# Attention, mixture of experts and a second feed-forward on one core: C's maxima kept in PSUM, 1e-9 as the second addend of a sum, A's factor inside its multiplication, and new priorities

## The chip, the cores and the metric

The kernel runs on one core of a Trainium2 chip. The metric is device microseconds (us) of one execution, and the number to be predicted is the median of the runs of the changed kernel. The engines are TensorE (PE; its weight loads are PEld), VectorE (DVE), ScalarE (ACT), GpSimd (POOL) and SyncE (SP), which issues most of the DMAs. Every engine works through its own list of instructions in order.

## The reference, cut to what matters

Three parts run one after the other. The first is an attention with 32 landmarks per head, over 4 batches of 8 heads, 576 tokens and 64 columns:

```python
q_lm, k_lm = means of q and k over groups of 18 tokens      # 32 landmarks each
def sm(a, b):
    s = scale * a @ b.T
    e = np.exp(s - s.max(-1))
    return e / (e.sum(-1) + 1e-09)
A, Bm, C = sm(q, k_lm), sm(q_lm, k_lm), sm(q_lm, k)
Z = six Newton steps from Bm.T / (norms + 1e-6)             # an inverse of Bm
x = A @ Z @ C @ v
```

The result is one row of 512 per token. The second part gives each of the 2304 rows to the best of 8 experts (512 to 1024, relu, back to 512), scaled by the gate's probability, and an expert takes at most 576 rows. The third part is a feed-forward from 512 to 2048 and back with a slope alpha for negative values.

## The kernel before, in words

**Stages.** The attention is worked on in pieces of one batch b and half of the heads g (four heads, 128 partitions), eight pieces in all. For each piece `loads`, `turn` and `sums` fetch q and k, turn them on PE and form the landmarks; `attend_c` makes C, B and the product with v; `attend_a` makes A. `attention_post` then inverts B with six Newton steps on PE and DVE (tiles `RW`), first for batch 0 alone (`post0`), then for batches 1 to 3 together (`post`), and ends in `route`, which gives every row its expert and writes `table`. When batch 0's logits `L` are known, `first_expert` writes the number of an expert into `e0i`, and `weights` loads that expert's matrices with that number (tiles `W1` and `W2`, both shown as `W` in the profile). `landmark_rows` multiplies W1 by the landmark rows (`big<-W,MT` on PE) and splits the product into two 16-bit halves (`MW`).

**First pass and loop.** The first pass, written out in full, is `moe_h` (PE: `mm<-xT,MW`), `moe_y` (`mm<-W,hgA`), `moe2_h` (`mm<-yA,WIa` and `mm<-yB,WIa`) and `moe2_out` (`mm<-WO,hgA`, `mm<-WO,hgB`). Meanwhile the third part's 64-bit weights are narrowed (DVE, three instructions a pair of chunks: `WIa<-hgA`, `WIb<-st`, `W<-st`, `MW<-st`, `xT<-st`) and split (`WIa<-WIa,s_wi`, then `WO<-W,s_wo`). `experts` makes a list of the (batch, expert) pairs that are left (`x_lst`), and a loop runs the same four steps for each; the profile shows two turns of it.

**What sets the order.** Every sequence of operations is a stream with a rank. `Plan.run` picks, with costs of its own for every instruction, the operation that can start first; a stream of smaller rank may go ahead within `patience + EAGER * difference of ranks`. What comes out is one fixed order on each engine. Where the plan sees PE wait, `keep_warm` puts matmuls of zeros on PE's list ahead of the waiting work (tiles `zero` and `ones`; L1730 in the profile; below: fillers). They are part of the program: PE runs them whether or not the wait comes.

**What the change touches.** In `attend_c` (L673) the two maxima go into `mx`, are multiplied by `exps` into `nm2`, and ACT's two exponentials write their sums into `sums`; then 1e-9 is added (`rs<-sums`) and the reciprocal taken. In `attend_a` (L736) the sums of A go into `asum`, one instruction adds 1e-9 and multiplies by 1/64, then come the reciprocal and the multiplication of T1 (`T<-T,asum`). `moe_tiles` (L1134) makes the long-lived tiles, `mtn` among them, which the first `prefetch` writes. The numbers are at L25, L210 and in the calls that make streams. GpSimd's subtraction for the 16-bit remainder of A is the POOL instruction `parts<-AT,parts`.

Of the kernel before, what the change touches and what calls it, by code (L numbers as in the profile page):

```python
# [11 lines left out]
AF = mybir.ActivationFunctionType  # L12
ALU = mybir.AluOpType
AX = mybir.AxisListType
# [3 lines left out]
P = 128  # L18
# [6 lines left out]
RANKS = [[-190.251, -162.415], [-189.669, -24.286], [-21.570, 79.087], [95.553, -68.442]]  # L25
# [6 lines left out]
MUL = "dddddddd"  # L32
# [172 lines left out]
class Plan:  # L205
# [5 lines left out]
    EAGER = -23.848  # L211
# [173 lines left out]
class Kernel:  # L385
# [41 lines left out]
    def constants(self):  # L427
# [29 lines left out]
        self.streams["constants"].own = -182.905  # L457
# [72 lines left out]
    def loads(self):  # L530

        for b in range(self.B):
            for g in range(2):
                heads = slice(4 * g, 4 * g + 4)
                self.streams["loads"].own = RANKS[b][g] + -135.434
                for nm, src in (("k", self.k), ("q", self.q)):
                    self.raw[nm, b, g] = t = yield Get(self.S["qk"])
                    yield self.dq.dma_start(t, src[b, heads].rearrange("h (p j) d -> (h p) j d", j=TG))
                    self.have.add((nm, b, g))
                if (b, g) == (0, 0):  # L540
                    self.streams["values"] = yield Fork(self.values(), -141.457)

    def values(self):

        for b in range(self.B):
            for g in range(2):
                heads = slice(4 * g, 4 * g + 4)
                if (b, g) != (0, 0):
                    self.streams["values"].own = RANKS[b][g] + -72.894
                self.raw["v", b, g] = t = yield Get(self.S["v"])  # L550
                src = self.v[b, heads]
                yield self.dq.dma_start(t[:, :, :4].rearrange("p h t d -> p h (t d)"), src[:, : 4 * P].rearrange("h (p t) d -> p h (t d)", t=4))
                yield self.dq.dma_start(t[:64, :, 4], src[:, 4 * P :].rearrange("h p d -> p h d"))
                self.have.add(("v", b, g))
                if (b, g) == (0, 0):
                    self.tc.prologue_barrier()

    def sums(self):
# [3 lines left out]
        for b in range(self.B):  # L562
            for g in range(2):
                self.streams["sums"].own = RANKS[b][g] + -193.537
# [24 lines left out]
    def turn(self):  # L589
# [8 lines left out]
        for b in range(self.B):  # L598
            for g in range(2):
                self.streams["turn"].own = RANKS[b][g] + -168.287  # L600
# [71 lines left out]
    def attend_c(self, b, g):  # L672
# [4 lines left out]
        def t(name, n):  # L677
            return self.ap.tile([P, n], F32, tag=name, name=f"{name}{b}{g}", bufs=dict(sums=4, rs=4, EB=3).get(name, 2))
# [7 lines left out]
        mx, nm2, sums, rs, EB = t("mx", 2), t("nm2", 2), t("sums", 2), t("rs", 2), t("EB", 32)  # L686
# [5 lines left out]
        yield act.activation(EC.rearrange("p (m j w) -> p m j w", m=LM, w=2), turned, AF.Exp, bias=nm2[:, 0:1], scale=0.125 / TG, accum_out=sums[:, 0:1])  # L692
        yield act.activation(EB, landmarks, AF.Exp, bias=nm2[:, 1:2], scale=0.125 / TG**2, accum_out=sums[:, 1:2])
        yield Put(big)
        yield dve.tensor_scalar(rs, sums, 1e-9, None, op0=ALU.add)
# [38 lines left out]
    def attend_a(self, b, g):  # L734
# [15 lines left out]
        amx, asum = t("amx", 18), t("asum", 18)  # L750
# [16 lines left out]
        self.streams["store", b, g] = yield Fork(self.store(b, g, parts), -169.245)  # L767
# [8 lines left out]
    def attention_post(self, bs):  # L776
# [79 lines left out]
        if b == 0:  # L856
            self.streams["post0"].own = -65.619
# [53 lines left out]
        for n, bb in enumerate(bs):  # L911
# [18 lines left out]
            if bb == 0:  # L930
                yield from self.first_expert(L[0:1, 0, 0, :])
                self.streams["post0"].own = -141.092
            yield Fork(self.used(bb, AT))
        self.have.add(("x", bs[-1]))
        if b:
            yield self.until(("routed", 0))
            self.streams["post"].own = -137.701
# [37 lines left out]
    def route(self, bs, L):  # L975
# [82 lines left out]
        if b == 0:  # L1058

            i0 = self.ar.tile([P, 5], F32, tag="r_i0", name="r_i0")  # L1060
            yield dve.scalar_tensor_tensor(i0, code[:, 0], self.e0c, row[:, 0], op0=ALU.is_equal, op1=ALU.mult)
            yield dve.tensor_scalar(self.idx0, i0, float(self.NT), None, op0=ALU.add)
            self.have.add("idx0")
            self.streams["post0"].own = 87.367
# [68 lines left out]
    def moe_tiles(self):  # L1133
# [12 lines left out]
        self.mtn = t("mtn", [P, 2, 2, 32])  # L1146
        self.gate, self.gn = t("gate", [P, self.B, 5]), t("gn", [P, 5])
# [55 lines left out]
    def landmark_rows(self, MT, slots, late=0.0):  # L1203
# [26 lines left out]
        scale = yield Fork(self.scale_of("w1", 4), -169.035)  # L1230
# [38 lines left out]
    def early(self):  # L1269
# [12 lines left out]
        self.streams["early_loads"] = yield Fork(loads(), 95.023)  # L1282
# [42 lines left out]
    def convert(self, name, n, amax=None, low="d", load=None, first=0):  # L1325
# [9 lines left out]
        scale = yield Fork(self.scale_of(name, n // 2, amax), -176.626)  # L1335
# [12 lines left out]
    def weight2(self, name, src, amax, low, first=0):  # L1348
# [9 lines left out]
        if name == "wi":  # L1358
            self.streams["wi_loads"] = yield Fork(self.fetch(name, src, range(first, 16, 2), arrived), -164.840)
        else:  # L1360
            self.streams["wo_loads"] = yield Fork(self.fetch(name, src, range(first, 16, 2), arrived), -192.828)
# [248 lines left out]
    def pre(self):  # L1610

        yield self.until(("P", 0, 0), ("P", 0, 1), *([("used", self.n_early - 4)] if self.n_early else ["early"]))
        self.streams["first"].own = -176.600
# [4 lines left out]
        self.streams["first"].own = -137.454  # L1618
# [3 lines left out]
        self.streams["first"].own = -135.600  # L1622
# [3 lines left out]
    def weights(self):  # L1626
# [4 lines left out]
        self.streams["rows"] = yield Fork(self.landmark_rows(self.MT[:, 0:2], [self.big] * 2), -69.061)  # L1631
        yield self.until("early")
        self.streams["weights"].own = -23.924
        yield from self.load_expert(bass.ds(e0, 1), ["w2"])
        self.streams["weights"].own = -139.397
# [85 lines left out]
    def run(self):  # L1721
# [15 lines left out]
        with tc.manual_schedule(engines={ET.PE, ET.DVE, ET.Activation, ET.Pool, ET.SP}):  # L1737
# [24 lines left out]
            for _ in range(10):  # L1762
# [5 lines left out]
                "constants": Stream(self.constants(), -68.342),  # L1768
                "post0": Stream(self.attention_post([0]), -168.986),
                "first": Stream(self.pre(), -79.218),  # L1770
                "weights": Stream(self.weights(), 79.632),
                "rooms": Stream(self.rooms(), -66.559),
                "post": Stream(self.attention_post(list(range(1, self.B))), -164.819),
                "early": Stream(self.early(), 71.164),
                "wi": Stream(self.weight_in(), -75.754),
                "wo": Stream(self.weight_out(), -66.781),
                "clear": Stream(self.clear(), -178.670),
                "experts": Stream(self.experts(), -70.639),
                "out": Stream(self.first_out(), -183.331),
                "next": Stream(self.first_next(), -135.603),  # L1780
                "next_w1": Stream(self.next_w1_late(), -193.387),
                "next_w2": Stream(self.next_w2('d'), -168.460),
            }
            for b in range(self.B):
                for g in range(2):
                    self.streams["c", b, g] = Stream(self.attend_c(b, g), RANKS[b][g] + -75.228)
                    self.streams["a", b, g] = Stream(self.attend_a(b, g), RANKS[b][g] + 80.769)
# [41 lines left out]
```

## Time and profile before

| | |
|---|---|
| median of 3 runs | 524.16 us (523.25 to 524.59) |
| the profiled execution | 524.16 us, of which the span in the trace is 519.9 us |
| busy in the span | PE 503.6 us, DVE 299.4 us, ACT 259.4 us, POOL 88.8 us |
| matmuls of zeros (L1730) | 174 in the first pass |
| first pass on PE | up to 248.13 us; then two turns of the loop, at 248.13 and 381.74 us |
| granted PE clock | 0.998 of full speed |

A profile names an instruction by the line that issued it, which is L81 for all that the plan orders, and by its tiles. The page's first part gives busy time by engine, the table of windows gives it by stretch of time, and a row of the timeline gives start, duration, engine, operation and, in brackets, the idle time ahead of it with what ended it.

### The profile page before, as it was taken

How to read it: one execution, taken by the hardware profiler on the slowest of the kernel's cores; microseconds unless marked ns; L12 is line 12 of the kernel's file. 1: busy time of each engine (PE TensorE's matmuls, PEld its weight loads, DVE VectorE, ACT ScalarE, POOL GpSimd, SP SyncE). 2: the span in 40 equal slices, each digit the busy share in tenths (PEclk: the TensorE clock that was granted, in tenths of full speed). 3: DMA queues.
4: the chain of work that ended last, by engine and by line, in shares of the span. 5: the costliest groups of instructions: out<-in, count | busy, mean ns of one | idle time of the engine just before them, and what ended most of it. 6: DMA issues, size and time to landing. Idle time of an engine off the chain costs nothing.

```text
span 519.9 us, 12146 instructions
## 1 busy us (share of the span) xinstructions
PE 503.6 (97%) x4809; PEld 332.0 (64%) x4809; DVE 299.4 (58%) x712; ACT 259.4 (50%) x579; POOL 88.8 (17%) x139
## 2 busy tenths in 40 slices
PE   8999999999989999999999999999999999999995
PEld 6777867776576774444755868644575587774444
DVE  6888989989999988024422657900033356682000
ACT  5666575774687676533522568700132255881000
POOL 4979401010134332011100000000100000000001
PEclk9999999999999999999999999999999999999999
DMA  8897597526553596500013570000000249000000
GB/s 309 303 331 244 172 276 264 182 103 223 151 143 143 185 308 207 202 34 29 33 20 52 155 242 0 1 21 20 20 30 0 50 94 317 3 0 2 38 20 32
DMA packets 50682, 64.47 MB, mean 124 GB/s; under 512 B 20320, under 2 KB 34032, under 8 KB 50640
## 3 DMA queue, kind: packets, MB, share of 16 engines
q1 hardware_dynamic: 49536, 60.34, 36.8%
q0 software_dynamic: 1104, 3.54, 1.8%
q8 instruction: 30, 0.49, 0.4%
q14 instruction: 12, 0.10, 0.1%
HBM read 49.50 MB, written 10.62 MB: 116 GB/s over the span
## 4 chain that ended last, share of the span: by engine, by line
PE 79%; DVE 9%; issue 6%; DMA 4%; ACT 1%; POOL 0%; POOLq 0%; SPq 0%; ACTq 0%; DVEq 0%
PE mm L81 73%; PE big L81 4%; PE mm L1730 2%; DVE WIa L81 2%; DMA out<-st,idxc 2%; DVE W L81 1%; DVE MW L81 1%; DMA st<-in_moe_w_out 1%; DVE mm L81 1%; DVE hgA L81 1%; DMA qk<-in_k 1%; DVE g L81 1%; ACT st L81 0%; PE big L1730 0%; ACT MW L81 0%
## 5 line engine op out<-in xcount | busy, mean ns | idle before, releaser
L81 PEld LDWEIGHTS <-hgA 128*128 128x128 f16 (+1 forms) x864 | 70.5, 102 | 69.2 <-issue 6.2
L81 PEld LDWEIGHTS <-WIa 128*128 128x128 f16 x864 | 84.2, 98 | 28.2 <-issue 6.7
L81 PE MATMUL mm<-WO,hgA 128*128 128x512 f16 (+1 forms) x432 | 72.8, 344 | 0.0
L81 PE MATMUL mm<-W,hgA 128*128 128x512 f16 (+1 forms) x432 | 72.7, 344 | 0.2
L81 PE MATMUL mm<-WO,hgB 128*128 128x512 f16 (+1 forms) x432 | 72.8, 344 | 0.0
L81 PE MATMUL mm<-yB,WIa 128*128 128x320 f16 x432 | 61.5, 299 | 1.8 <-DVE hgA L81 1.2
L81 POOL DMA_INDIRECT out<-st,idxc x12 | 12.3, 1028 | 287.9 <-ACT st L81 282.8
L81 PEld LDWEIGHTS <-hgB 128*128 128x128 f16 (+1 forms) x432 | 35.3, 102 | 36.1 <-issue 3.3
L81 ACT ACTIVATE st<-mm,fac 128x512 f32<-128x512 f32 (+1 forms) x15 | 9.7, 644 | 97.6 <-PE mm L81 97.4
L81 PE MATMUL mm<-yA,WIa 128*128 128x256 f16 x432 | 50.6, 272 | 2.3 <-DVE g L81 1.7
L81 ACT ACTIVATE g<-mm 128x256 f32<-128x256 f32 (+1 forms) x96 | 39.2, 413 | 20.9 <-PE mm L81 14.8
L81 DVE SCALAR_TENSOR_TENSOR mm<-g,oma,mm 128x256 f32<-128x256 f32 (+1 forms) x80 | 40.9, 517 | 8.2 <-ACT g L81 7.5
L81 PE MATMUL mm<-xT,MW 128*128 128x320 f16 (+1 forms) x288 | 37.0, 286 | 1.8 <-ACT st L81 1.8
L81 PEld LDWEIGHTS <-MW 128*128 128x128 f16 x288 | 27.6, 98 | 9.3 <-ACT st L81 1.4
L81 PEld LDWEIGHTS <-WIb 128*128 128x128 f16 x288 | 28.2, 99 | 7.1 <-issue 0.2
L81 ACT ACTIVATE junk<-mm 128x512 bf16<-128x512 f32 (+1 forms) x27 | 15.5, 573 | 34.4 <-PE mm L81 34.2
L81 DVE COPY idxc<-idxn 128x5 int32<-128x5 int32 x2 | 0.3, 172 | 54.9 <-issue 43.9
L81 ACT COPY qkT<-mm 128x512 f32<-128x512 f32 (+1 forms) x48 | 22.6, 525 | 17.1 <-PE mm L81 17.0
L81 ACT ACTIVATE junk<-W 128x1024 bf16<-128x1024 f32 x21 | 22.2, 1055 | 8.7 <-DMA W<-in_moe_w 8.2
L81 ACT ACTIVATE hgA<-mm 128x256 f16<-128x256 f32 (+1 forms) x48 | 19.5, 409 | 13.7 <-PE mm L81 13.4
L81 DVE TENSOR_TENSOR hgA<-mm,hgA 128x256 f16<-128x256 f32 (+1 forms) x40 | 18.2, 455 | 14.1 <-ACT hgA L81 13.3
L81 DVE SCALAR_TENSOR_TENSOR hgA<-mm,hgA 128x256 f16<-128x256 f32 (+1 forms) x48 | 20.9, 454 | 7.5 <-ACT hgA L81 7.3
(286 smaller groups left out, 751.5 us busy)
## 6 DMA issues: line engine op xcount, KB each, us to landing
W<-in_moe_w SPq DMA_DIRECT2D x8, 1024.0 KB, 8.6
st<-in_moe_w_out SPq DMA_DIRECT2D x16, 512.0 KB, 4.3
hgA<-in_moe_w_in SPq DMA_DIRECT2D x10, 512.0 KB, 6.9
qk<-in_k SPq DMA_DIRECT2D x8, 576.0 KB, 5.4
qk<-in_q SPq DMA_DIRECT2D x8, 576.0 KB, 6.4
out<-zero SPq DMA_DIRECT2D x18, 256.0 KB, 4.3
v<-in_v SPq DMA_DIRECT2D x8, 512.0 KB, 5.4
W<-in_moe_w SPq DMA_DIRECT2D x8, 512.0 KB, 5.6
```

Source lines behind the costliest of these rows:

```text
L81: r = getattr(self.lane.engine, name)(*a, **k)
L1730: nc.tensor.matmul(o[:, :256], self.ones16, self.zero.bitcast(F16), start=True, stop=True)
```

## The change

C: both maxima are written into two unused columns of the same PSUM tile (`SC[:, 1008:1010]`), and the multiplication reads them there. The sums of C, and those of A, go into the first place of pairs whose second place holds 1e-9, written once at the start into `mtn`; a `tensor_reduce` over each pair then adds it. A: the factor 64 goes into the multiplication of T1, which becomes a `scalar_tensor_tensor`. All ranks, `RANKS` and `EAGER` have new values.

```diff
-RANKS = [[-190.251, -162.415], [-189.669, -24.286], [-21.570, 79.087], [95.553, -68.442]]
+RANKS = [[-158.429, -51.160], [-190.869, -58.900], [-50.798, 57.716], [-188.686, -53.152]]
-    EAGER = -23.848
+    EAGER = -192.112
...
-        mx, nm2, sums, rs, EB = t("mx", 2), t("nm2", 2), t("sums", 2), t("rs", 2), t("EB", 32)
+        nm2, rs, EB = t("nm2", 2), t("rs", 2), t("EB", 32)
+        mx, sums = SC[:, 1008:1010], self.sums2[:, 2 * b + g]
...
-        yield act.activation(EC.rearrange("p (m j w) -> p m j w", m=LM, w=2), turned, AF.Exp, bias=nm2[:, 0:1], scale=0.125 / TG, accum_out=sums[:, 0:1])
+        yield act.activation(EC.rearrange("p (m j w) -> p m j w", m=LM, w=2), turned, AF.Exp, bias=nm2[:, 0:1], scale=0.125 / TG, accum_out=sums[:, 0, 0:1])
...
-        yield dve.tensor_scalar(rs, sums, 1e-9, None, op0=ALU.add)
+        yield dve.tensor_reduce(rs, sums, axis=AX.X, op=ALU.add)
         yield dve.reciprocal(rs, rs)
...
-        yield dve.tensor_reduce(asum, T13, axis=AX.X, op=ALU.add)
-        yield dve.tensor_scalar(asum, asum, 1e-9, 1.0 / ASCALE, op0=ALU.add, op1=ALU.mult)
+        yield dve.tensor_reduce(asum2[:, :, 0], T13, axis=AX.X, op=ALU.add)
+        yield dve.tensor_reduce(asum, asum2, axis=AX.X, op=ALU.add)
         yield dve.reciprocal(asum, asum)
-        yield (dve if MUL[2 * b + g] == "d" else self.gp).tensor_tensor(T13, T13, asum.unsqueeze(2).to_broadcast([P, 18, 32]), op=ALU.mult)
+        yield dve.scalar_tensor_tensor(T13, T13, ASCALE, asum.unsqueeze(2).to_broadcast([P, 18, 32]), op0=ALU.mult, op1=ALU.mult)
...
+        eps = self.mtn.rearrange("p g k m -> p (g k m)")[:, :104]
+        self.nc.vector.memset(eps, 1e-9)
+        self.asum2 = eps[:, :72].rearrange("p (g n a) -> p g n a", g=2, a=2)
+        self.sums2 = eps[:, 72:].rearrange("p (g n a) -> p g n a", n=2, a=2)
...
-                "weights": Stream(self.weights(), 79.632),
+                "weights": Stream(self.weights(), -189.922),
```

The new numbers move most instructions of the first pass, on every engine; the loop's order is the same but for two instructions near its end. Two places bear on the prediction. The first is on DVE, where the first logits are copied (`L`) and the first expert's number is written (`e0i`). Before, `AT` tiles of batch 2 are being made there and the row stands 121st of DVE's rows:

```order
L81 COPY L_1135<-mm_1136 128x40
L81 TENSOR_SCALAR rs_1128<-sums_1127 128x2
...
L81 SCALAR_TENSOR_TENSOR WIa<-hgA,WIa 128x1024
L81 TENSOR_REDUCE m_1265<-d_1266 1x1
L81 STREAM_TRANSPOSE AT_1288<-T_5_966 128x576
L81 TENSOR_SCALAR e0i<-m_1265 1x1
L81 TENSOR_REDUCE r_mx_1337<-L_1135 128x5
```

Of the changed kernel, at the same two instructions (`T_8` is the last of the eight pieces of A, `Bn` the three later batches' B):

```order
L80 COPY L_1401<-mm_1402 128x40
...
L80 TENSOR_REDUCE m_1452<-d_1453 1x1
L80 STREAM_TRANSPOSE T_8_1387<-big_1433 128x576
L80 TENSOR_SCALAR e0i<-m_1452 1x1
L80 TENSOR_REDUCE rsum_1515<-Bn_131 128x6
L80 TENSOR_SCALAR a_1483<-a_1483 1x1
L80 TENSOR_REDUCE amx_1510<-T_8_1387 128x18
```

The first expert's number now comes behind nearly all of the attention's DVE work, 147th instead of 121st of the rows.

The second place is on DVE in the first `moe2_h`, from the second activated product on (`mm<-g,oma,mm` and `g<-g,oma,mm` are the products' slopes, `hgA` their low halves, `W<-st` a narrowing of w_out, `WIa<-WIa,s_wi` a split of w_in). Before:

```order
L81 SCALAR_TENSOR_TENSOR g_2_2660<-g_2_2660,oma,mm_2640 128x256
L81 SCALAR_TENSOR_TENSOR xh_2548<-mm_2497,pys,xh_2548 128x2x256
...
L81 TENSOR_TENSOR hgA<-mm_2613,hgA 128x256
L81 SCALAR_TENSOR_TENSOR WIa<-WIa,s_wi 128x2x512
L81 SCALAR_TENSOR_TENSOR mm_2676<-g_3_2692,oma,mm_2676 128x256
L81 COPY x_n<-mm_2679 32x2
L81 SCALAR_TENSOR_TENSOR W_86<-st_6_2468,W_86 128x1024
L81 SCALAR_TENSOR_TENSOR g_4_2714<-g_4_2714,oma,mm_2697 128x256
```

Of the changed kernel, from the same product (`SS` and `tsum` belong to the routing of batches 1 to 3):

```order
L80 SCALAR_TENSOR_TENSOR g_2_2625<-g_2_2625,oma,mm_2604 128x256
...
L80 TENSOR_SCALAR W_86<-st_7_2489 128x1024
L80 TENSOR_TENSOR tsum<-tsum,SS 128x8
...
L80 TENSOR_TENSOR hgA<-mm_2589,hgA 128x256
L80 SCALAR_TENSOR_TENSOR mm_2638<-g_3_2654,oma,mm_2638 128x256
L80 SCALAR_TENSOR_TENSOR g_4_2686<-g_4_2686,oma,mm_2661 128x256
L80 CAST SS<-tsum 128x8
L80 SCALAR_TENSOR_TENSOR W_86<-st_7_2489,W_86 128x1024
```

The splits of w_in now stand ahead of the stretch, and in their place stand small instructions of the later batches' routing, which before stood ahead of it.

## Rows read from the trace of the kernel before

**Rows 1.** The page's part 1: busy time by engine.

```profile
PE 503.6 (97%) x4809; PEld 332.0 (64%) x4809; DVE 299.4 (58%) x712; ACT 259.4 (50%) x579; POOL 88.8 (17%) x139
```

**Rows 2.** Windows: stretch and length, then busy PE, PEld, DVE, ACT, POOL, clock, DMA.

```profile
0.00:52.00 52.00, 49.02 (x786) 37.99 (x786) 41.92 (x96) 32.32 (x83) 39.12 (x95) 1.00 0.86 297
52.00:97.00 45.00, 43.49 (x798) 33.72 (x798) 41.44 (x116) 26.68 (x65) 8.34 (x9) 1.00 0.70 230
97.00:144.00 47.00, 47.00 (x606) 31.32 (x604) 45.10 (x111) 31.88 (x61) 4.77 (x3) 1.00 0.53 167
144.00:210.00 66.00, 62.49 (x463) 44.34 (x460) 59.15 (x110) 45.84 (x95) 21.33 (x18) 1.00 0.64 200
```

**Rows 3.** What PE waited for, 0 to 210: total us, times, longest.

```profile
PE mm L81 <- DVE g L81: 2.3, 3, 1.1
PE mm L81 <- DVE hgA L81: 1.2, 2, 0.8
PE big L81 <- DVE nm L81: 1.1, 1, 1.1
...
PE mm L1763 <- PEq L1814: 0.8, 1, 0.8
PE mm L81 <- DVE WIa L81: 0.8, 1, 0.8
```

**Rows 4.** Fillers: one stretch of the chain of waits.

```profile
81.96 2.40 PE mm L1730 x21
```

**Rows 5.** DVE, groups by shape, 0 to 110: count, busy us, mean ns.

```profile
L81 DVE SCALAR_TENSOR_TENSOR WIa<-hgA,WIa 128x1024 int32<-128x1024 int32 x10 | 12.9, 1290 | 0.0
L81 DVE TENSOR_TENSOR T<-T,amx 128x576 f32<-128x576 f32 x8 | 6.7, 843 | 0.0
...
L81 DVE TENSOR_REDUCE mx<-big 128x1 f32<-128x576 f32 x8 | 6.0, 755 | 2.3 <-PE big L81 2.3
...
L81 DVE TENSOR_REDUCE asum<-T 128x18 f32<-128x576 f32 x8 | 5.9, 739 | 0.6 <-ACT T L81 0.5
L81 DVE TENSOR_SCALAR rs<-sums 128x2 f32<-128x2 f32 x8 | 3.5, 442 | 1.0 <-ACT EB L81 0.8
L81 DVE TENSOR_SCALAR WIa<-hgA 128x1024 int32<-128x1024 int32 x5 | 3.4, 674 | 0.0
...
L81 DVE TENSOR_SCALAR asum<-asum 128x18 f32<-128x18 f32 x8 | 2.2, 275 | 0.0
...
L81 DVE TENSOR_TENSOR nm<-mx,exps 128x2 f32<-128x2 f32 x8 | 2.1, 258 | 0.0
```

**Rows 6.** Timeline, DVE and POOL: a slow and a quick addition of 1e-9.

```profile
42.18 0.17 DVE L81 TENSOR_SCALAR rs<-sums 128x2 f32<-128x2 f32 x1
...
59.69 1.50 POOL L81 TENSOR_TENSOR parts<-AT,parts 128x576 f16<-128x576 f32 x1 [3.58 <-ACT parts L81]
...
60.08 1.14 DVE L81 TENSOR_SCALAR rs<-sums 128x2 f32<-128x2 f32 x1
```

**Rows 7.** DVE, groups by shape, 100 to 210.

```profile
L81 DVE SCALAR_TENSOR_TENSOR W<-st,W 128x1024 int32<-128x1024 int32 x10 | 14.6, 1461 | 0.0
L81 DVE SCALAR_TENSOR_TENSOR WIa<-WIa,s_wi 128x1024 f16<-128x1024 f32 x3 | 3.8, 1277 | 0.0
L81 DVE SCALAR_TENSOR_TENSOR xh<-mm,pys,xh 128x512 f16<-128x512 f32 x4 | 3.0, 743 | 0.0
L81 DVE TENSOR_TENSOR table<-table,rows 128x40 f32<-128x40 f32 x3 | 0.6, 195 | 0.0
```

**Rows 8.** Timeline: first expert's number, the load that uses it, its product on PE.

```profile
64.52 0.10 DVE L81 TENSOR_SCALAR e0i<-m 1x1 int32<-1x1 f32 x1
...
67.96 1.86 SPq L81 DMA_DIRECT2D W<-in_moe_w  x3
...
76.97 0.65 PE L81 MATMUL big<-W,MT 64*32 64x512 f32 x4
```

**Rows 9.** DMA issues, 60 to 80: KB each, median us from issue to landing.

```profile
W<-in_moe_w SPq DMA_DIRECT2D x4, 128.0 KB, 5.7
```

More of the change, by code (lines that the diff above doesn't have):

```diff
@@ L31 @@
 SUB = "dddddddd"
-MUL = "dddddddd"
 LOW1 = "dpdpdpdp"
@@ L534, in loads @@
                 heads = slice(4 * g, 4 * g + 4)
-                self.streams["loads"].own = RANKS[b][g] + -135.434
+                self.streams["loads"].own = RANKS[b][g] + -157.874
                 for nm, src in (("k", self.k), ("q", self.q)):
@@ L563, in sums @@
             for g in range(2):
-                self.streams["sums"].own = RANKS[b][g] + -193.537
+                self.streams["sums"].own = RANKS[b][g] + 54.323
                 i = 2 * b + g
@@ L749, in attend_a @@
         T13 = T1.rearrange("p (c m) -> p c m", m=32)
-        amx, asum = t("amx", 18), t("asum", 18)
+        amx, asum, asum2 = t("amx", 18), t("asum", 18), self.asum2[:, g]
         yield dve.tensor_reduce(amx, T13, axis=AX.X, op=ALU.max)
@@ L856, in attention_post @@
         if b == 0:
-            self.streams["post0"].own = -65.619
+            self.streams["post0"].own = -181.017
         big = yield Get(self.big)
@@ L1612, in pre @@
         yield self.until(("P", 0, 0), ("P", 0, 1), *([("used", self.n_early - 4)] if self.n_early else ["early"]))
-        self.streams["first"].own = -176.600
+        self.streams["first"].own = -186.359
         yield from self.moe_h(True)
@@ L1617, in pre @@
         yield self.dve.tensor_copy(self.idxc, self.idx0)
-        self.streams["first"].own = -137.454
+        self.streams["first"].own = -187.258
         yield from self.moe_y((0, 1, 2, 3, 4), self.gate[:, 0], True)
@@ L1621, in pre @@
         yield self.until("rooms")
-        self.streams["first"].own = -135.600
+        self.streams["first"].own = -150.662
         yield from self.moe2_h(True)
@@ L1630, in weights @@
         yield from self.load_expert(bass.ds(e0, 1), ["w1"])
-        self.streams["rows"] = yield Fork(self.landmark_rows(self.MT[:, 0:2], [self.big] * 2), -69.061)
+        self.streams["rows"] = yield Fork(self.landmark_rows(self.MT[:, 0:2], [self.big] * 2), 48.870)
         yield self.until("early")
-        self.streams["weights"].own = -23.924
+        self.streams["weights"].own = -187.066
         yield from self.load_expert(bass.ds(e0, 1), ["w2"])
-        self.streams["weights"].own = -139.397
+        self.streams["weights"].own = -155.098
         yield from self.convert("w2", 8, low='d')
@@ L1767, in run @@
                 "sums": Stream(self.sums(), 2),
-                "constants": Stream(self.constants(), -68.342),
-                "post0": Stream(self.attention_post([0]), -168.986),
-                "first": Stream(self.pre(), -79.218),
-                "weights": Stream(self.weights(), 79.632),
[L1772 to L1782, printed above, removed]
+                "constants": Stream(self.constants(), 57.961),
+                "post0": Stream(self.attention_post([0]), -158.428),
+                "first": Stream(self.pre(), -58.855),
+                "weights": Stream(self.weights(), -189.922),
+                "rooms": Stream(self.rooms(), 49.798),
+                "post": Stream(self.attention_post(list(range(1, self.B))), -157.914),
+                "early": Stream(self.early(), 58.474),
+                "wi": Stream(self.weight_in(), -51.944),
+                "wo": Stream(self.weight_out(), 50.277),
+                "clear": Stream(self.clear(), 58.542),
+                "experts": Stream(self.experts(), -189.913),
+                "out": Stream(self.first_out(), -153.589),
+                "next": Stream(self.first_next(), -188.874),
+                "next_w1": Stream(self.next_w1_late(), -153.665),
+                "next_w2": Stream(self.next_w2('d'), -58.892),
             }
```

32 lines of the change are left out of this document (16 added, 16 removed).

## The prediction

> **What bounds the kernel now.** I began with the page's busy times: PE works for 503.6 us of a span of 519.9 us, no other engine for more than 299.4 us [rows 1]. So the end moves only by what PE has to do and by the gaps between its matmuls. The profiled execution took 524.16 us, 4.3 us more than its span, and is itself the median of the three runs, so the sum below needs no correction. The change is in the first pass alone: the loop keeps its order but for two instructions, and its two turns take 133.6 us each in the profile. I cut the first pass into windows [rows 2] to see where PE has gaps: 52.00 - 49.02 = 2.98 us, 1.51 us, none, and 3.51 us from 144 on, 8.0 us in all before 210. The clock column reads 1.00 in all of them, so no slower clock hides in these figures. Then I read the list of PE's waits to see who ends the gaps [rows 3]: DVE's products `g` and `hgA` (2.3 + 1.2 = 3.5 us, the whole gap of the fourth window), DVE's `nm` (1.1), PE's own sequencer at the start (0.8) and a first narrowed weight (0.8). The last two stay, since nothing that precedes them is touched. At most 8.0 - 1.6 = 6.4 us can go. DVE is the late one: from 97 to 144 it is busy for 45.10 of 47 us while PE never stops [rows 2].
>
> **PE's own work.** The matmuls are the same but for the fillers. The plan now writes 179 of them where it wrote 174. Before, 21 took 2.40 us, 0.114 us each [rows 4]. Five more add **0.57 us** to PE's list; nothing hides that, because PE is the bound and runs them whether the wait comes or not.
>
> **The small DVE instructions.** Eight additions of 1e-9 in C took 0.442 us each, eight of `asum` 0.275, eight `nm` 0.258 [rows 5]. The timeline shows what the long ones hold: at 42.18 such an addition took 0.17 us, at 60.08 it took 1.14 us and ended with GpSimd's subtraction, which ran from 59.69 to 61.19 [rows 6]. So I take 0.17 as the price free of GpSimd, for each of the three kinds, and read the rest as waiting for GpSimd's use of the memory that both reach. The new forms (a reduction over pairs, a multiplication that reads PSUM) don't occur in the trace. Their nearest rows are reductions: `asum<-T`, with both ends in SBUF, took 0.739 us, and `mx<-big`, which reads as many columns from PSUM, 0.755 [rows 5], and neither mean holds anything like the added microsecond. If the new forms run free, DVE saves 8 x (0.27 + 0.105 + 0.09) = 3.7 us; if they are held as long as the old ones, nothing. I take 3.7 us, by the nearness to those reductions. That is DVE's work, not yet PE's time: it shortens the end only where a gap is waiting.
>
> [...] The rows put a PSUM source 0.016 us above an SBUF source (0.755 to 0.739) [rows 5], 0.1 us over the eight `nm`. [...]
>
> Other edits cost little. One fill of 1e-9 is added ahead of all work, for at most the 0.17 us of another small instruction, while DVE waits for its first load. C's second maximum now waits for the first, since both write one tile; the first is needed for `nm` anyway. A's multiplication by the sum's reciprocal has two operands as before and takes the factor with it: no difference (bounds: 0.807 us, its mean before, against 0.843 for its sister `T<-T,amx` [rows 5], 0.3 us over eight).
>
> **The moved work.** In the fourth window DVE sheds the three splits of w_in, one narrowing of w_out and one `xh`: 3 x 1.277 + 1.461 + 0.743 = 6.0 us [rows 7]. In their place come 17 small instructions of the later batches' routing; at the 0.195 us of `table` [rows 7] these are 3.3 us. Net, DVE has 2.7 us less to do between the first product and the last, and the waits for `g` and `hgA` sit there [rows 3]. What left goes into the window before, where DVE had only 47 - 45.10 = 1.9 us free [rows 2]; it fits because of the 3.7 us from the small instructions. Both halves are needed. With them PE's gap of 3.5 us shrinks by **2.7 us** (bounds: 0 and 3.5; PE has as much to do ahead of the first `yA` as before, within 0.1 us). What is late next is the same DVE with 0.8 us to go. The third part's tokens are now listed (`x_lst`) behind this stretch, but SP still writes zeros to the output then, so the next expert's load starts no later: nothing.
>
> In the first two windows the change shortens what precedes `nm` in one piece by 0.27 + 0.105 + 0.09; the wait of 1.1 us for it [rows 3] falls by **0.5 us** (bounds: 0 and, were every movable gap there closed, 2.9).
>
> **The sum.** 524.16 + 0.57 - 2.7 - 0.5 = **521.5 us**. With all 6.4 us gone it would be 518.3.
>
> **Rival: the first expert's weights come late.** `e0i` stood 121st on DVE and stands 147th. Ahead of it come twelve more whole-tile instructions of A at 0.739 to 0.843 us (9.5), three more narrowings at 1.290 and two first steps at 0.674 (5.2), and some 1.7 of small ones; off goes what the pieces already ahead save (6 x 0.27 + 5 x 0.105 + 6 x 0.09 = 2.7) and about 0.7 of index arithmetic that is moved behind it: 13 us more [rows 5]. Before, `e0i` was written at 64.52 and PE multiplied W1 at 76.97, 12.45 us later, with no wait there [rows 8]. The loads are issued up to 69.82, and one lands 5.7 us after its issue [rows 8, 9], so the chain needs between (67.96 + 5.7 - 64.52 =) 9.1 and 11.0 us, and at most 12.45. PE's list ahead of that product has grown by 7.9 us, 3.6 of it from fillers that were moved there (52 now, 20 before, since the first logits), so PE arrives at about 84.9. If DVE only adds the 13 us, `e0i` comes at 77.5, the weights at 86.6 to 90.0, and PE waits 1.7 to 5.1 us, say 3.4. From `e0i` later than about 74 to 76 on this decides. DVE would then wait as well: behind the product stand its halves `MW`, and behind them the narrowings, so the gain of the fourth window is lost, too. Time: 524.73 + 3.4 = **528.1 us**, slower. For it: the plan itself fills the place with zeros, as if it saw a wait. Against it: DVE had some 11 us idle ahead of `e0i` (64.5 us, less 41.92 of work up to 52 and 12.5 x 41.44 / 45.00 = 11.5 after that [rows 2]), which more work can fill; if half of it is filled, `e0i` comes at 72 and nothing waits.
>
> **Rival: the relief is passed on.** GpSimd's 1.50 us subtraction still runs [rows 6], and DVE's two-operand instructions on whole tiles (`T<-T,amx`, the narrowings) still follow closely. If the next of them is held in place of the small one, DVE saves nothing, the 2.7 us moved ahead overfill the third window, and PE's wait only moves from the fourth window to the first product: 524.16 + 0.57 = **524.7 us**, no change that counts. This is also the case in which the change doesn't do what it says. For it: both engines' lists keep those instructions. Against it: these large ones show means close to a reduction's (0.843 and 0.739 [rows 5]), so they have seldom been held. [...]
>
> **Rival: nearly all gaps close.** If DVE's 3.7 us run ahead through all windows, the 6.4 us go but for one: 524.73 - 5.4 = **519.3 us**. Against it: the gaps at `nm` stand behind a chain through PE, ACT and DVE that shorter additions don't wholly remove.
>
> **Chances.** About 0.3% (1.6 us) is what a measurement of this kernel tells from no change: faster means below 522.6, slower above 525.7. My forecast, 520.5 to 522.6, has 0.29; nearly all gaps closed 0.18; the relief passed on, up to half of the forecast's gain with it, 0.24; the late weights 0.29, of which a fifth is short waits near no change. So faster 0.47, same 0.24 + 0.06 = 0.30, less 0.05 for small losses elsewhere = 0.25, slower 0.23 + 0.05 = 0.28. The range goes from 518.3, the floor, to 528.3, just above the late weights' middle; outside are only their upper half and surprises.
>
> **What would show it.** In the new profile: the pair sums at 0.17 us or less, with none near 1 us while GpSimd subtracts; PE's waits for `g` and `hgA` together at 0.8 us and the fourth window's gap shrunk as much; `e0i` before about 75 and no wait at `big<-W,MT`; 179 fillers; loop turns of 133.6 us. A wait of 2 us or more at `big<-W,MT` would make the first rival right, and a DVE as busy as before from 97 to 144 with the gap moved to the first product the second. The prediction is wrong in its reasoning, even at the right time, if the gain comes from the loop or from PE's list.

## The result and the profile after

The changed kernel took **530.09 us** (median of 4 runs, 527.7 to 531.4) against 523.7 us of the kernel before in the same runs: a ratio of 1.0108, 95% interval 1.0074 to 1.0142. It is slower, by more than the range of the prediction allowed (up to 528.3 us). A second set of runs gave 531.45 us and 1.0127 (1.0081 to 1.0172).

The profiled execution is the quickest of the four, 527.7 us at a granted clock of 1.000. The other three took 529.33, 530.84 and 531.4 us at 0.996, 0.992 and 0.992. So the loss has two parts: some 3.5 us that this execution shows against the 524.16 us of before, and 2 to 3 us more, in executions with a lower clock.

The windows of the changed kernel answer to [rows 2], with the same columns:

```profile
0.00:52.00 52.00, 47.45 (x686) 38.17 (x686) 45.77 (x93) 33.48 (x77) 37.33 (x68) 1.00 0.94 333
52.00:97.00 45.00, 44.01 (x933) 32.41 (x932) 38.33 (x112) 26.82 (x70) 18.45 (x38) 1.00 0.61 187
97.00:144.00 47.00, 44.84 (x513) 30.47 (x513) 42.58 (x93) 32.85 (x61) 5.01 (x2) 1.00 0.51 159
144.00:210.00 66.00, 63.13 (x508) 46.09 (x506) 60.54 (x134) 44.54 (x96) 16.80 (x17) 1.00 0.65 195
```

PE's gaps are now 4.55, 0.99, 2.16 and 2.87 us, 10.6 us in place of 8.0. The new ones stand ahead of 144 us: the third window, where PE never stopped before, has 2.2 us. The list of what PE waited for from 0 to 210 (total us, times, longest) answers to [rows 3]:

```profile
PE mm L80 <- issue: 2.0, 2, 1.8
PE mm L80 <- DVE WIa L80: 1.7, 1, 1.7
PE mm L1734 <- DVE y L80: 1.6, 1, 1.6
PE big L1734 <- DVE T L80: 1.4, 2, 1.2
PE mm L80 <- DVE g L80: 1.1, 1, 1.1
...
PE mm L1734 <- ACT MT L80: 0.6, 1, 0.6
```

The wait for `hgA` in the fourth window is gone and that for `g` is less than half; a wait for `y` of 1.6 us is there instead, one for `T` in place of that for `nm`, the first wait for `WIa` is 0.9 us longer, and 2.0 us are put down to "issue", to nothing that the profile knows of. Two waits of before that [rows 3] leaves out, 0.9 us for `MW` and 0.5 for `EB`, are gone. The loop begins at 252.00 us where it began at 248.13, and its first turn takes 133.5 us, as before; the whole difference is made in the first pass. Of the 3.87 us, 2.7 are gaps of PE (the two lines below) and 0.57 the five fillers (179 are run); the rest is the first `big<-W,MT`, which took 1.72 us in place of 1.14. PE's time up to the loop, before and after (length, busy, clock, DMA):

```profile
0.00:248.13 248.13, 239.52 (x2909) 1.00 0.61 200
0.00:252.00 252.00, 240.73 (x2915) 1.00 0.61 196
```

The first `mm<-yA,WIa` comes 4.4 us later than before (148.46 for 144.08), so the later half of the first pass even gains 0.5 us.

The small instructions on DVE did what was forecast, and others grew (DVE, groups by shape, 0 to 115, as [rows 5]):

```profile
L80 DVE SCALAR_TENSOR_TENSOR WIa<-hgA,WIa 128x1024 int32<-128x1024 int32 x10 | 13.9, 1386 | 0.0
L80 DVE TENSOR_TENSOR T<-T,amx 128x576 f32<-128x576 f32 x8 | 7.5, 931 | 0.0
L80 DVE SCALAR_TENSOR_TENSOR T<-T,asum 128x576 f32<-128x576 f32 x8 | 7.3, 913 | 0.0
...
L80 DVE TENSOR_SCALAR WIa<-hgA 128x1024 int32<-128x1024 int32 x5 | 4.4, 879 | 0.0
...
L80 DVE TENSOR_REDUCE asum<-mtn 128x18 f32<-128x36 f32 x8 | 1.4, 176 | 0.0
...
L80 DVE TENSOR_REDUCE rs<-mtn 128x2 f32<-128x4 f32 x8 | 1.1, 138 | 0.2 <-ACT EB L80 0.2
L80 DVE TENSOR_TENSOR nm<-big,exps 128x2 f32<-128x2 f32 x8 | 1.0, 128 | 0.0
```

`rs`, `asum` and `nm` fell from 7.8 us together [rows 5] to 3.5, by 4.3 us where 3.7 was forecast. But the two narrowings, `T<-T,amx` and `T<-T,asum` grew by 3.5 us (1.0 + 1.0 + 0.7 + 0.8, the last from 0.807 us each before), and up to the loop DVE was busy 196.8 us in all, 196.4 before.

### The profile page after: what moved, and what is told of

Read it like the earlier page. It is cut to its first block, busy times and chain, and to the rows that moved or that the text cites. A ratio compares the mean times of both kernels' runs of the same rounds, so it can differ in the third digit from the quotient of the medians.

```text
span 523.7 us, 12153 instructions
## 1 busy us (share of the span) xinstructions
PE 504.8 (96%) x4814; PEld 333.6 (64%) x4814; DVE 299.7 (57%) x713; ACT 260.5 (50%) x579; POOL 93.1 (18%) x139
## 4 chain that ended last, share of the span: by engine, by line
PE 80%; DVE 8%; issue 7%; DMA 3%; ACT 1%; POOL 0%; POOLq 0%; ACTq 0%; DVEq 0%
PE mm L80 74%; PE big L80 3%; PE mm L1734 3%; DVE WIa L80 2%; DMA out<-st,idxc 2%; DVE W L80 1%; DVE T L80 1%; DMA qk<-in_k 1%; PE big L1734 1%; DVE big L80 1%; DVE xh L80 0%; DVE mtn L80 0%; DVE tsum L80 0%; ACT st L80 0%; DVE AT L80 0%
```

## Operations or order

The change does two things at once, so they were taken apart. A kernel's picks (which stream's operation goes next, and how many fillers ahead of it) were written down and put into the other kernel as a list `ORDER`, with the numbers that belong to it:

```diff
-            s = min(ready, key=lambda s: (s.start, s.rank))
-            while True:
...
+            k, self.n_fill = ORDER.pop(0)
+            s = next(x for x in ready if x.key == k)
...
-        n = max(int((start - t - 100) // 108), min(8, int((4000 - recent) // 256)))
...
+        for i in range(self.n_fill):
+            self.fill(self.tiles[name])
```

Each engine then has the other kernel's order, instruction by instruction. The later experiments move rows of such a list or change its counts of fillers.

**New operations, old order** (`new_ops_old_order`).

> The changed operations of A and C, but every engine's list in exactly the order of the kernel before (recorded and written in as a list), with its 174 fillers. Theory 1 (the order does the harm; the operations give a little, because DVE waits less for GpSimd): 521 to 523.7 us. Theory 2 (the new operations do harm, for example C's second maximum that waits for the first, or the PSUM operands): above 525 us. Theory 3 (the relief is passed on whole to other instructions): within 1 us of the kernel before, with the pair sums near 0.15 us and T<-T,amx, T<-T,asum, WIa<-hgA longer than before by as much in sum.

Measured: 524.25 us against 524.46, ratio 0.9997 (0.9975 to 1.0020). The operations alone change nothing. What PE waited for from 0 to 211 in it:

```profile
PE mm L80 <- DVE g L80: 2.3, 3, 1.1
PE mm L80 <- DVE hgA L80: 1.2, 2, 0.8
PE big L80 <- DVE nm L80: 1.1, 1, 1.1
```

These are the rows of before [rows 3] to the tenth. In this kernel `rs`, `asum` and `nm` take 4.2 us less, all of DVE's groups up to the loop together 2.6 us less; so 1.6 us went to other instructions (`T<-T,amx` from 0.843 to 0.891 us, the first step of the narrowings from 0.674 to 0.895), and the 2.6 us that DVE did save were not what PE waited for. Theory 3 is nearest, though the relief was passed on by less than half.

**Old operations, new order** (`old_ops_new_order`).

> The operations of the kernel before in exactly the order of the changed kernel, with its 179 fillers. Theory 1 (the order does the harm): 528 to 533 us, as slow as the changed kernel or slower, since DVE also loses the shorter sums. Theory 2 (the operations do the harm): near 524 us. Theory 3 (relief passed on whole): within 1 us of the changed kernel.

Measured: 532.26 us (530.57 to 534.9), ratio 1.0136 (1.0078 to 1.0193). Theory 1: the order does the harm, all 6 to 8 us of it.

**The changed kernel again** (`changed_again`).

> The changed kernel itself, run again. Its profiled execution took 527.7 us at a granted clock of 1.000, its other three executions 529.33 to 531.4 us at 0.992 to 0.996. Theory (two parts): about 3.6 us of the loss are gaps and fillers in the first pass, present in each execution, and a further 1.6 to 3.7 us, in most executions, come with a stretch of lower granted clock. Then this run shows 527.5 to 531.5 us again, the time rising as the mean clock falls. Rival: the low clock was chance of that chip; then all executions stand near 527.7 us at 1.000.

Measured: 528.89, 531.42, 531.48 and 532.95 us, at clocks of 0.990 to 0.992. In the 19 runs of the kernel before that stand beside these, 522.78 and 522.93 us go with a clock of 1.000 and 526.3 and 526.58 us with 0.993; the median is 524.46 us at 0.997. The theory's two parts are there: 3.5 to 4.9 us at the full clock (527.7 less 522.8 to 524.2, what the kernel before took at 1.000 in all sets), and some 2 us in executions with a lower one. But its second part is not shown by these four times: they differ by 4 us at nearly one mean clock, and the longest, at 0.992, lies above the range.

## A stop in the middle of a product

The 1.83 us put down to "issue" lie inside one product, between its 13th and 14th matmul (timeline of the changed kernel, PE):

```profile
95.60 0.42 PE L80 MATMUL mm<-v,CT 128*32 128x64 f32 x13
97.84 0.77 PE L80 MATMUL mm<-v,CT 128*32 128x64 f32 x27 [1.83 <-issue]
```

The same instruction stops in all five profiles of the new order whose loads stand as in the changed kernel and whose fillers are all there, for 1.83 to 2.95 us. In the changed kernel PE had then run 1616 matmuls and 1617 weight loads; the next, small stop comes at 103.22 us after 1744 and 1745 (counts of matmuls from windows up to just before either stop):

```profile
0.00:97.54 97.54, 91.47 (x1616) 1.00 0.79 265
0.00:102.92 102.92, 96.54 (x1744) 1.00 0.80 271
```

That is 3233 and 3489 instructions, 256 apart. The DMA view shows a queue of its own for them: one packet of 0.02 MB on "q8 instruction" at 95.5 us, in a quarter of a microsecond in which the engines are 100.8% taken by the loads of W2 and w_in; in the kernel before the like packet at 95.25 us had the engines to itself. The DMA view of the changed kernel, 95.50 to 95.75 (packets, MB, share of the engines' time):

```profile
q1 hardware_dynamic: 48, 0.09, 100.8%
q8 instruction: 1, 0.02, 24.7%
```

The same view of the kernel before, 95.25 to 95.50, which shows that queue alone:

```profile
q8 instruction: 1, 0.02, 24.0%
```

From 0 to 130 us the same view counts 16 such packets in the changed kernel, and PE runs 2064 matmuls and 2065 weight loads in that time, 258 instructions for a packet, near the 256 between the two stops. Here the crossing of such a border cost up to 3.3 us (`after_half`, below).

Is it `e0i`? It was written at 77.00 us, and SP had sat idle for it:

```profile
77.00 0.10 DVE L80 TENSOR_SCALAR e0i<-m 1x1 int32<-1x1 f32 x1
...
78.16 6.58 SPq L80 DMA_DIRECT2D W<-in_moe_w  x8
...
85.77 1.72 PE L80 MATMUL big<-W,MT 64*32 64x512 f32 x16
...
89.96 1.09 PE L80 MATMUL big<-W,MT 64*32 64x512 f32 x16
```

`big<-W,MT` began 8.8 us after `e0i`, with no wait ahead of it. Inside it the weight loads (PEld) sat 0.5 us for `W`, so that it took 0.6 us more than its second half; that is what the late `e0i` cost on PE. But the loads queued on SP behind `e0i` (v, W2, w_in) come one upon the other from 84.8 us on, when PE runs its smallest instructions.

**`e0i` earlier** (`e0_early`). The six DVE rows move up:

```
 TENSOR_TENSOR nm<-big,exps 128x2
+COPY L<-mm 128x40
+TENSOR_REDUCE m<-L 1x1
...
+TENSOR_SCALAR e0i<-m 1x1
 SCALAR_TENSOR_TENSOR WIa<-hgA,WIa 128x1024
...
```

> The changed kernel with one move on DVE: the copy of the first logits and the five instructions up to e0i stand directly behind nm of the last piece, 3 to 4 us earlier; all other orders stay. Theory (the late e0i holds SP, so that the loads of W1, v, W2 and w_in pile up behind it and PE's program page, fetched among them, comes late: the stop of 1.83 us inside mm<-v,CT): e0i near 73.5 us, the stop at mm<-v,CT under 0.8 us, time 1 to 2 us less than the changed kernel. Rival (the stop has nothing to do with e0i): stop and time unchanged within 0.5 us.

Measured: 528.38 us (526.25 to 530.95 in nine of the ten runs, the tenth 535.04), ratio 1.0067 (1.0036 to 1.0099), 1.7 to 3.1 us less than the changed kernel, whose interval it overlaps. The stop is there as ever, 2.12 us at the same matmul. In its profile `e0i` came at 75.4 us only, 1.6 us earlier than before the move: this execution was 0.9 us behind by then, and DVE had to wait 0.88 us for PE's logits. The median fits, the stop does not: moving all loads together doesn't part them from PE's program.

**Fewer instructions ahead of the border** (`fewer_on_page`): four entries of the list, the fillers ahead of the second half of `big<-W,MT` and of three products behind it.

```diff
-('weights/1landmark_rows', 15)
+('weights/1landmark_rows', 0)
...
-('attention_post.123', 9)
-('weights/1landmark_rows/5scale_of.4', 1)
+('attention_post.123', 0)
+('weights/1landmark_rows/5scale_of.4', 0)
...
-('attention_post.123', 7)
+('attention_post.123', 0)
```

> The changed kernel without the 32 fillers (64 PE instructions) that stand from the first big<-W,MT to the last mm<-v,CT; everything else stays. Theory (PE's program arrives in pieces of 256 instructions; the piece that begins 13 matmuls into the last mm<-v,CT comes late because PE runs through the piece before it in 4.0 us while the DMA engines are full): with 64 instructions fewer the border moves 64 instructions on, mm<-v,CT runs through without a stop, and a stop, if any, stands 64 instructions later and is under 1 us; time 1.5 to 3 us below the changed kernel's 530 to 531.5. Rival (mm<-v,CT waits for its data, v or CT): the stop of 1.8 to 2.8 us stays inside mm<-v,CT, and the time stays within 1 us.

Measured: 530.87 us, no gain. `mm<-v,CT` ran through, as the theory had it, and the stop stands at the same count, after 1615 matmuls, which is now 64 instructions further on in the work; but it is not smaller, it is 2.86 us (PE's timeline):

```profile
102.31 0.18 PE L80 MATMUL mm<-r_oh,tail_main 128*128 128x32 f16 x1 [2.86 <-issue]
```

So the stop belongs to the border and not to `v` or `CT`. The kernel with half of the fillers (`after_half`, below) says the same: there 1615 matmuls and 1616 weight loads end within another product, and PE stops in it:

```profile
98.84 0.42 PE L80 MATMUL mm<-RW 32*32 32x64 f32 x4 [3.31 <-issue]
```

**The loads later** (`loads_later`).

```diff
+        yield self.dq.dma_start(self.held, self.sc["w1"][0][0:1, 0:1])
         yield from self.load_expert(bass.ds(e0, 1), ["w2"])
```

> The changed kernel with the two loads of W2 and the w_in loads behind them held back on SP until DVE has written the scale s_w (about 95 us in place of 90.5), by a 4-byte store of s_w ahead of them. PE's list and all others stay. Theory (the stop inside the last mm<-v,CT is a piece of PE's program that waits behind those loads): the stop falls from 1.8 to 2.8 us to under 0.7 us, at the same instruction or none, and the time by 1 to 3 us unless W2 is now late. Rival (the stop comes from PE's own rate of instructions alone): the stop stays at 1.8 us or more.

Measured: the stop is gone, and the product runs as one. The only row of PE put down to "issue" in this stretch is one of 0.26 us, after 1489 matmuls and as many weight loads, so at the border before (2978 instructions; 3233 less 256 is 2977):

```profile
95.78 1.05 PE L1786 MATMUL mm<-zero,ones 128*128 128x256 f16 x8 [0.26 <-issue]
...
99.48 0.90 PE L80 MATMUL mm<-v,CT 128*32 128x64 f32 x40
```

This shows the cause: a piece of PE's program stood behind the loads of W2 and w_in, since PE's own list is the same. In the seven profiles with the stop, PE goes on 2.2 to 2.5 us after the packet of its program starts (in the changed kernel's at 97.84 after 95.61 us), whatever the length of the stop: the later that packet comes beside the border, the longer PE stands. The time is 529.1 us (526.76 to 533.77), ratio 1.0096 (1.0051 to 1.0141), 1.0 to 2.4 us less than the changed kernel, which these spreads don't tell from nothing. W2, asked for at 99.5 us where 95 had been expected, is now late in turn: ACT waits 1.74 us for it, and PE 2.23 us for the `hgA` that stands behind on ACT.

## An addition held by GpSimd

In the fourth window the wait for `y` is this (timeline of the changed kernel, 152 to 157 us):

```profile
153.09 2.41 POOL L80 TENSOR_TENSOR WIb<-WIb 128x1024 f16<-128x1024 f32 x1 [9.10 <-ACT WIb L80]
...
153.42 2.10 DVE L80 TENSOR_TENSOR tsum<-tsum,SS 128x8 f32<-128x8 f32 x1
...
155.45 0.47 DVE L80 SCALAR_TENSOR_TENSOR y<-mm,pys,y 128x256 f16<-128x256 f32 x1
```

`tsum` adds 8 columns, 0.16 us of work. It is one of the 17 small instructions of the later batches' routing that the new order puts here, and it ends with GpSimd's split; `y` stands behind it on DVE, and PE behind `y`. Another instruction of that routing, `r_oh<-r_m,dsc`, took 2.15 us at 141.98, ahead of this stretch (0.28 before), while GpSimd's `WIa<-WIa` ran from 141.10 to 143.99. Like the slow addition of [rows 6], `tsum` ends with GpSimd's instruction, at 155.52 and 155.50 us; what the two share while it is held, no run shows.

**`tsum` first** (`tsum_first`).

```
 CAST SS<-tsum 128x8
-TENSOR_SCALAR W<-st 128x1024
 TENSOR_TENSOR tsum<-tsum,SS 128x8
+TENSOR_SCALAR W<-st 128x1024
 SCALAR_TENSOR_TENSOR y<-mm,pys,y 128x256
```

> The changed kernel with one move on DVE in moe2_h: tsum<-tsum,SS (128x8) and y<-mm,pys,y stand ahead of the W<-st that was ahead of them; nothing else moves. Theory (tsum, 2.10 us in the changed kernel against 0.16 elsewhere, is held by GpSimd's WIb<-WIb, and y behind it, for which PE waits 1.56 us, with it): tsum near 0.16 us, PE's wait for y under 0.4 us, time 1 to 1.6 us under the changed kernel. Rival (y is late for its own reason, ACT's half): the wait stays over 1 us. Since single executions differ by 3 us with the clock, the waits decide rather than the median.

On DVE `tsum` alone went ahead; `y` still stands behind `W<-st`, other than the text before the run says.

Measured: this `tsum` 0.17 us (0.65 at most, at another place), and no wait for `y` (PE, 120 to 215):

```profile
PE mm L80 <- DVE g L80: 1.1, 1, 1.1
PE mm L80 <- DVE hgA L80: 1.1, 2, 0.6
PE mm L80 <- DVE xh L80: 0.3, 1, 0.3
```

That GpSimd's split held `tsum` is shown (2.10 us beside it, 0.17 ahead of it), but two thirds of the gain went to waits for `hgA` (0.5 and 0.6 us) further on. What GpSimd's split holds now is a small instruction further on, `fac`, which takes 0.20 us elsewhere and here 1.70, and `hgA` stands behind it (timeline, POOL and DVE):

```profile
156.29 0.17 DVE L80 TENSOR_TENSOR tsum<-tsum,SS 128x8 f32<-128x8 f32 x1
...
156.46 2.60 POOL L80 TENSOR_TENSOR WIb<-WIb 128x1024 f16<-128x1024 f32 x1 [9.10 <-DVE tsum L80]
...
157.38 1.70 DVE L80 SCALAR_TENSOR_TENSOR fac<-gate,pyr,wfac 128x1 f32<-128x1 f32 x1
```

The median, 530.0 us (4 runs, 527.29 to 530.46), can't tell 0.5 us.

## Mended together

**Three moves** (`mended`): those of `e0_early`, `loads_later` and `tsum_first` in one list.

> The changed kernel with three moves together: e0i 3.6 us earlier, the loads of W2 and w_in behind s_w, tsum and y ahead of W<-st. PE's list is unchanged. Theory (late e0i with its loads, the held tsum, and the clock lost after their stops are most of the loss of 6 to 7 us): 525 to 527.5 us, a clock of 0.994 or more. Rival (the order is slower by the sum of many small gaps): above 528 us.

Measured: 530.67 us (527.92 to 534.93): the rival's side. No stop at the border, no wait for `y`, but ACT sat in front of W2, and the first `hgA` behind it, and PE behind that (timeline):

```profile
100.61 1.06 ACT L80 ACTIVATE junk<-W 128x1024 bf16<-128x1024 f32 x1 [1.54 <-DMA W<-in_moe_w]
...
102.54 2.12 PE L80 MATMUL mm<-xT,MW 128*128 128x256 f16 x18 [2.03 <-DVE hgA L80]
```

**With ACT mended** (`mended2`): three `junk<-W` rows one to three places later on ACT.

```
-ACTIVATE junk,ss_w<-W 128x1024
 ACTIVATE hgA<-mm 128x256 x2
+ACTIVATE junk,ss_w<-W 128x1024
```

> The kernel with the three moves together (e0i earlier, W2 and w_in loads behind s_w, tsum and y ahead of W<-st), and on ACT the sums of squares of W2 (junk<-W) one to three places later, behind the first hgA. In that kernel PE waited 2.03 us for the first hgA, since ACT sat 1.54 us before junk<-W for the delayed W2. Theory (the stops of 1.5 to 3 us, and the clock after them, make the loss, and each mend had only passed it to the next one): PE's wait for the first hgA under 0.6 us, no stop over 1.3 us before the loop, 525 to 527.5 us. Rival (the new order's loss lies in many small gaps and in PE's instructions, whatever the large stops): above 528 us.

Measured: 531.1 us (529.54 to 532.21), ratio 1.0140 (1.0112 to 1.0169). The wait at the first `hgA` fell to 0.49 us, and two others took its place (what PE waited for, 0 to 212):

```profile
PE mm L80 <- DVE hgA L80: 3.1, 5, 1.4
PE mm L1786 <- ACT MT L80: 1.7, 1, 1.7
...
PE mm L80 <- DVE WIa L80: 1.2, 1, 1.2
```

The theory of a few large stops falls as an account of the whole loss. Each stop is real and each mend took it away, but a gap that closes at one place opens at the next: PE's gaps up to the loop sum to 11.1 us in this profile, 11.3 in the changed kernel's first. Beyond them its clock stood below 1.00 from 72 to 80 us, behind no stop, and from 108 to 116, behind these two waits, and PE's busy time up to the loop is 2.8 us longer (243.56 for 240.73).

## Clock and fillers

In the profiles with lower clock the fall can be placed. In the one of `changed_again` it follows the stop, which was 2.78 us there (windows; length, PE's busy time, clock, DMA):

```profile
96.00:100.00 4.00, 1.45 (x38) 0.94 1.01 399
100.00:104.00 4.00, 4.00 (x65) 0.63 0.82 286
```

A mean of 0.63 lies between the full clock and the 0.50 of the lowest such stretch (`after_half`, 72 to 76 us, with PE busy throughout); over 4 us it costs 0.37 of them, 1.5 us. The mean over a whole execution tells less: in `before` (0.998) and `new_ops_old_order` (0.995) a clock below 1.00 stands only behind PE's last matmul, from 517.7 and 518.2 us on, where it costs nothing. Of the ten profiles in the new order (the half-filled one below among them), seven show such a stretch between 96 and 116 us, behind a gap of 1.2 to 3.3 us; six show one between 68 and 84 us, where PE had not waited over 0.2 us for over 20 us; some show both, and one, the changed kernel's first, neither. Of the four profiles in the old order with all or half of the fillers, one shows any, at 8 to 16 us.

**Half of the fillers, old order**, with the new operations (`half_fillers`) and with the old (`old_ops_half`): in the list, each count `n` becomes `n // 2`, 78 fillers in place of 174.

> A try at a faster version: the new operations in the order of the kernel before, each run of fillers halved (78 in place of 174). Theory 1 (part of the fillers run where PE's work was ready, so they cost PE time): 519 to 523 us. Theory 2 (they stand in waits that come anyway): 523.5 to 525 us with PE gaps in their place. Theory 3 (the gaps lower the granted clock): above 525.5 us, the clock below 0.995.

> The kernel before, its operations and order as they are, each run of fillers halved (78 in place of 174). Theory (the gain of the halved version comes from the fillers alone, none from the new operations): 520.5 to 522.7 us, as with the new operations. Rival (half of that gain comes from the new operations' relief): 523 to 524 us.

Measured: 521.63 us, ratio 0.9946 (0.9923 to 0.9970), and 520.83 us, ratio 0.9945 (0.9922 to 0.9967). **Both are faster than either kernel**, and the new operations add nothing here either. Of `old_ops_half`, PE up to the loop:

```profile
0.00:244.81 244.81, 231.32 (x2814) 1.00 0.64 202
```

Against the kernel before PE is busy 8.2 us less (by the price of 0.114 the 96 fillers would be 10.9), and its gaps grow from 8.6 to 13.5 us, by 4.9; the difference, 3.3 us, is the part of the fillers that stood where work was ready.

**None** (`no_fillers`).

> The new operations in the order of the kernel before, without any filler in the first pass (0 in place of 174; halved, they gave 521.6 us). Theory 1 (each filler costs PE time where work is ready, and gaps of under 2 us cost no clock): 518 to 521 us. Theory 2 (without them PE's gaps bring the clock down): above 523 us, with the clock under 0.99 and stretches at half clock before 110 us in the profile.

Measured: 523.18 us (520.84 to 526.38), ratio 0.9978 (0.9952 to 1.0005), at clocks of 0.978 to 0.991. Theory 2, if only just: PE has fewer instructions, but the clock falls where they stood:

```profile
80.00:84.00 4.00, 1.93 (x20) 1.00 0.88 351
84.00:88.00 4.00, 1.70 (x80) 0.59 0.65 205
88.00:92.00 4.00, 3.17 (x81) 0.50 1.00 378
```

**Half, new order** (`after_half`), 77 in place of 179.

> The changed kernel with each run of fillers halved (77 in place of 179). Halving gave 3.4 us in the old order. Theory (half of the fillers run where PE's work is ready, here as there): 526.5 to 528.5 us. Rival (this order needs them for the clock): 530 us or more, with the clock under 0.99.

Measured: 524.74 us (523.85 to 526.67), ratio 1.0015 (0.9998 to 1.0032); 5 to 7 us less than the changed kernel, more than either theory had, though the stop at the border is 3.3 us long in it and its clock (0.986 to 0.996) is no better. So the new order's fillers cost it 2 to 3 us more than those of the old order cost there. The order as such still costs 3.9 us against `old_ops_half`, 3.1 against `half_fillers`, which has the same operations. PE up to the loop in this profile:

```profile
0.00:250.22 250.22, 235.91 (x2813) 0.98 0.61 198
```

The loop begins 5.4 us later than in `old_ops_half`. Only 0.8 us of that are gaps (14.3 for 13.5); 4.6 us are PE's longer busy time for one matmul less, and PE's clock is below 1.00 from 68 to 80 and from 96 to 104 us here, nowhere before the loop there. In these two profiles most of what is left of the loss is clock.

## Why the prediction was wrong

521.5 us was forecast, 530.09 measured. The step that failed leads from DVE's work to PE's gaps: the sum took 2.7 + 0.5 us off the gaps, because DVE would have that much less to do; PE's gaps up to the loop grew by 2.7 us instead (8.6 to 11.3). The terms, one by one:

- **What bounds the kernel**: right. The end moved by PE's gaps in the first pass, its fillers and its clock; the loop's turns stayed.
- **Fillers, +0.57 us**: the count was right, 179. That their place matters was not weighed: 52 of them stand between the first logits and `big<-W,MT`, and halving all gave 5 to 7 us in this order.
- **Small instructions, -3.7 us of DVE**: right, -4.3 us. For `nm` from PSUM the rows gave 0.016 us more; measured were 0.128 and 0.135 us each, no more than the 0.17 taken as free of GpSimd, and the quickest took 0.097, from SBUF 0.120. What failed is the next step, that they carry PE's gaps: with the old order they took nothing off PE's waits.
- **First two windows, -0.5 us**: failed. In the old order the wait for `nm` stayed 1.1 us, and in the new order one for `T` of 1.2 replaced it, with 0.9 more at the first `WIa`. That `WIa` is not a narrowed weight, as the prediction read it, but holds sums for the landmarks: its product starts 0.3 us later (9.74 for 9.42), with w_in's first loads now among q and k, and the fillers ahead of it ended 0.6 us sooner. Gaps of 4.5 us were forecast near 4.0, and are 5.5, 1.0 of it the first half of the stop at the border.
- **The fourth window, -2.7 us**: failed, and it is the largest term. Its gap fell from 3.5 to 2.9 us. DVE did lose the work: from the first `mm<-yA,WIa` to the first `mm<-WO,hgA` it was busy 46.6 us, 49.1 before. But it was not what PE waited for, one for one. The 17 small instructions were priced at 0.195 us from one row, at a place where GpSimd was idle; one of them took 2.10, held by GpSimd, ahead of `y`, and PE got a wait of 1.6 us for a product that it had not waited for.
- **The third window**, where the sum had only moved work fit in: it got 2.2 us of gaps: 1.0 at borders of PE's program, 0.84 of it with the DMA engines 99% taken, which no row of before showed as a wait, the rest at `MT`, `hgA` and `tot_w`.
- **The late weights**: `e0i` came at 77.0 (forecast 77.5), PE at 85.8 (84.9), and the first weights within 8.8 us, less than the 9.1 to 11.0 taken, so `big<-W,MT` lost 0.6 us, not 3.4. The rival's sign was right and its time (528.1) is near by luck; the loads behind `e0i` on SP cost more, by the stop of 1.83 us.
- **The relief passed on**: the mechanism is there, about 1.6 of 4.2 us with the old order, and all of it in the new one; it costs nothing by itself, as that rival had it. Against it the prediction said that the large ones have seldom been held; the trace of before has one that took long beside GpSimd, a narrowing of 2.13 us at 33.27 (1.21 in the median), while `xT<-AT,xT` ran from 32.69 to 34.32.
- **The clock**: the sum took 1.00 throughout, as the one profile showed. Nine of the ten profiles in the new order have one to three stretches of lower clock before the loop, some 1.5 us each, the old order's with all fillers none: 2 us in most runs that no term held.

What stays open: why the clock fell at 68 to 84 us, where PE had not waited, why it falls in so many executions of the new order, and which of its many moves brings which gap.

## What to carry to other kernels

Take a change of operations and a new schedule apart by writing the old order down and replaying it; here that showed within two runs that one was worth nothing and the other cost 7 us. Price a moved instruction by who runs beside it at its new place, above all a small one beside a long instruction of GpSimd (here 2.10 us in place of 0.16), and ask what stands behind it on its engine. Fillers are work on the engine that bounds the kernel: halve them and measure before anything subtler.

## What was not expected of the hardware

- PE stopped at borders of its program 256 of its instructions apart (after 3233 and 3489 of them), and a packet on the DMA queue "q8 instruction" came 2.2 us before it went on; with the loads ahead of that packet (the DMA engines 100.8% taken in the changed kernel's profile) such a stop took 1.8 to 3.3 us in the midst of a product, and with the loads held back (`loads_later`) 0.26 us.
- An addition of 128x8 took 2.10 us beside a GpSimd instruction of 2.41 us, 0.16 us elsewhere; moved ahead of it, it took 0.17, and an instruction of 128x1 behind it 1.70 in place of 0.20.
- The granted clock fell behind stops of 1.2 us and more, but not behind each: those of 1.83, 2.12 and 2.38 us (the changed kernel's first profile, `e0_early`, `old_ops_new_order`) cost none.
